# Two attention blocks on one core: block A's finished rows are transposed by VectorE and a DRAM round trip instead of TensorE, and split by GpSimd

## The chip, the cores and the metric

The kernel runs on one core of one Trainium2 chip. TensorE (PE; its weight loads are shown apart as PEld), VectorE (DVE), ScalarE (ACT) and GpSimd (POOL) each work through a queue of instructions in order; SyncE (SP) issues nearly all DMAs, in order too. An instruction waits for what it reads, and everything queued behind it on its engine waits with it. The metric is the device time of one execution in microseconds, as the median of several runs; one more execution was profiled, and the profile's rows come from that one.

## The reference

Two attention blocks with the same shapes (one sequence of 2048 positions, width 640, 32 heads of 20), side by side in the output. Block A lets each position see eight earlier ones at a distance of two; block B is full attention.

```python
def _A_ref(x, wqkv, wo):                    # W, dil = 8, 2
    q, k, v = split_heads(x @ wqkv)
    idx = pos[:, None] - off[None, :]       # off = arange(8) * 2
    logits = einsum("bhsd,bhswd->bhsw", q, k[idx]) * Dh ** -0.5   # masked where idx < 0
    o = einsum("bhsw,bhswd->bhsd", softmax(logits), v[idx])
    return merge_heads(o) @ wo
def _B_ref(x, wqkv, wo):
    q, k, v = split_heads(x @ wqkv)
    o = softmax(q @ k.T * Dh ** -0.5) @ v
    return merge_heads(o) @ wo
return concatenate([a, b], axis=-1)
```

## The kernel before

**Stages.** First come block A's projections (queries, keys and values go to DRAM), then block B's, then the main loop of 514 steps, in which block B's attention runs, and last block B's output projection. Block A's attention is computed by GpSimd beside block B's work, from the B projections on to about four fifths of the main loop.

**The main loop.** `NS = 512` steps are the combinations of 8 groups of four heads, 4 blocks of 512 queries and 16 blocks of 128 keys; `LAG = 2` more steps drain it. In step `i`, `b_qk(i)` makes four score tiles (TensorE into a PSUM bank each, of which there are four in the ring `bank()`; ScalarE's exponential to SBUF frees the bank); `b_pv(i - 2)` multiplies the exponentials of an earlier step by the values; and `b_max(i + 24)` makes the scores of a later query block once more, transposed, in two pairs of banks (`wide()`, a ring of two), and VectorE takes each row's maximum (tile `mx`, two `TENSOR_REDUCE` a step). TensorE may fill a `wide()` pair only when VectorE has read what stood in it. Every second step ScalarE copies the accumulated values into one of four `more` buffers and GpSimd adds them to `braw`. For steps in `ALONE` (432 to 479) the order within a step differs (`b_both`).

**Program order.** Everything is issued in the order of the Python program (`InOrder`, line 56, keeps it; so every row of the profile carries line 56, and tiles tell them apart). `tick()` at the start of a step counts `now` up and runs what `after(n, fn, ...)` has put down for this step. `odd(n)` moves a time to an odd step of the loop; VectorE's small operations (`sm`, `mx1`, `am`, `mtr`) stand on odd steps.

**Block A's attention.** `UNITS` is a list of 128 units: for each of the `NT = 16` tiles of 128 rows, four units for the scores (`a_scores`) and four for the values (`a_values`); the four score units of tile t + 1 come ahead of the four value units of tile t. `a_work` does one unit per `next`, in the loop at `i % 14` in (1, 5, 7, 11), so eight units, one tile, in 28 steps; 13 units are done ahead of the loop. The tile's softmax (`a_softmax`) proceeds by one part with each unit; its reciprocal `am` on VectorE comes with the second unit after the last value unit of the tile before. The finished rows of a tile are `ao`, [128 rows, 640], and go into `done_a` with a count of 2 that goes down with each unit.

**Block A's output projection.** TensorE contracts over partitions, so the rows have to be turned: `aot` holds them as [128 columns, part, 5 chunks, 128 rows], in two parts, a rounded one and the rest (`hi` and `lo`), of which three products are added (`rows15`: 15 matmuls for 320 output columns). `out_piece()` runs in the loop at `i % 6 == 4` and does one piece of `a_out`: first the turn (five transposes by TensorE into a `wide()` pair, ScalarE's cast to `aot[:, 0]`, VectorE's subtraction to `aot[:, 1]`), then one half of the projection, then the other; so three pieces, 18 steps, a tile. When the last tile is out, the weights of block B's output are loaded (`WO_b`), which take the buffers of A's.

**Buffers.** `stg` is a ring of three tiles of [128, 640] that weights and loads are staged through; `aot` has one buffer.

Of the kernel before, what the change touches and what calls it, by code (L numbers as in the profile page):

```python
# [8 lines left out]
F32 = mybir.dt.float32  # L9
F32R = mybir.dt.float32r  # L10
AF = mybir.ActivationFunctionType
ALU = mybir.AluOpType
AX = mybir.AxisListType

D = 640
# [5 lines left out]
KC = 5  # L21
# [38 lines left out]
def attention_pair(ctx, tc, xa, wqk_a, wv_a, wo_a, xb, wqk_b, wv_b, wo_b, oa, ob):  # L60
# [3 lines left out]
    sb = ctx.enter_context(tc.tile_pool(name="sb", bufs=1))  # L64
    ps = ctx.enter_context(tc.tile_pool(name="ps", bufs=1, space=PS))
    dr = ctx.enter_context(tc.tile_pool(name="dr", bufs=1, space=bass.MemoryType.DRAM))
    pe, dve, act, gp, sp = (InOrder(tc, e) for e in (nc.tensor, nc.vector, nc.scalar, nc.gpsimd, nc.sync))


    now = [0]  # L70
    due = {}

    def after(n, fn, *args):
        due.setdefault(now[0] + n, []).append((fn, args))
# [7 lines left out]
    def tick():  # L82
        now[0] += 1
        for fn, args in due.pop(now[0], ()):
            fn(*args)
# [5 lines left out]
    def bank():  # L91

        n = free.pop(0)
        t = ps.tile([128, 512], F32, tag=f"st{n}", bufs=1, name="ps_st")
        taken[id(t)] = (n, t)
        return t

    def give(t):

        free.append(taken.pop(id(t))[0])  # L100

    def wide():

        return ps.tile([128, 2, 512], F32, tag="mx", bufs=2, name="ps_mx")
# [44 lines left out]
    def x_pieces(x, n, second=None):  # L149

        t = columns(n)
        src = x[:, n * 512:(n + 1) * 512].rearrange("(k p) c -> p k c", p=128)

        def piece(a, b):
            u = t[a // (KC - 1)]
            m = a % (KC - 1)
            split(u[:, 0, m:m + b - a], u[:, 1, m:m + b - a], src[:, a:b], "p", second)
        return t, [lambda a=a, b=b: piece(a, b) for a, b in PAIRS]

    def wide_pieces(src, second=None):  # L160

        w = [sb.tile([128, KC, 320], F32R, tag="w", bufs=4, name="ww") for _ in range(2)]
        return w, [lambda a=a, b=b: split(
            w[0][:, a:b], w[1][:, a:b], src[:, a:b], second=second, first=second and gp.tensor_copy) for a, b in PAIRS]
# [52 lines left out]
    def rows15(p, o, W):  # L217

        for k in range(KC):
            for i, (wi, xi) in enumerate(PASSES):  # L220
                pe.matmul(p[:, :320], o(xi, k), W[wi][:, k], start=(k == 0 and i == 0), stop=(k == KC - 1 and i == 2))
# [20 lines left out]
    def store_rows(p, dst):  # L242
        r = sb.tile([128, 320], F32, tag="r", bufs=3, name="ro")
        act.copy(r, p[:, :320])
        if id(p) in taken:
            give(p)
        after(1, sp.dma_start, dst, r)


    NT = S // 128  # L250
# [11 lines left out]
    t, more = x_pieces(xa, 1)  # L262
# [6 lines left out]
    for n in (2, 3):  # L269
        t, more = x_pieces(xa, n)  # L270
        XA.append(t)
        loads += more
    ident = const.tile([128, 128], F32, name="ident")
# [23 lines left out]
    UNITS = []  # L297
# [69 lines left out]
    next_a = [0]  # L367
    done_a = []

    def a_attention():  # L370
# [3 lines left out]
        for n, (t, c) in enumerate(UNITS):  # L374
# [17 lines left out]
            next_a[0] = n + 1  # L392
            yield

    def a_out(W):

        while done_a and done_a[0][0] <= 0:
            _, t, o = done_a.pop(0)
            ot = sb.tile([128, 2, KC, 128], F32R, tag="aot", bufs=1, name="aot")
            p = wide().rearrange("p b c -> p (b c)")  # L400
            for k in range(KC):
                pe.transpose(p[:, k * 128:(k + 1) * 128], o[:, k * 128:(k + 1) * 128], ident)
            pv = p[:, :D].rearrange("p (k c) -> p k c", c=128)
            act.copy(ot[:, 0], pv)
            dve.tensor_tensor(ot[:, 1], pv, ot[:, 0].bitcast(F32), ALU.subtract)
            yield
            for half in range(2):
                p = bank()
                rows15(p, lambda xi, k: ot[:, xi, k], W[half])
                store_rows(p, oa[t * 128:(t + 1) * 128, half * 320:half * 320 + 320])  # L410
                yield

    a_work = a_attention()
# [9 lines left out]
    for n in range(NA):  # L423
        nxt = None
        for t in range(NT):
            if n == 0 and t < 4:
                p = first[t]
            else:
                p = next(banks)
# [31 lines left out]
    def b_pieces(g):  # L461
        k = sb.tile([128, 2, S], F32R, tag="big", bufs=4, name="bk")
        q = sb.tile([128, NQC, 2, 512], F32R, tag="big", bufs=4, name="bq")
        v = sb.tile([128, NKB, VG], F32, tag="vb", bufs=2, name="vb")
        stacks[g] = (q, k, v)
        out = []
        hs = [slice(g * GH + 2 * r, g * GH + 2 * r + 2) for r in range(2)]

        def add(t, src, runs):
            for r0, s0, n in runs:  # L470
                out.append(lambda: sp.dma_start(t[r0:r0 + n].bitcast(F32), src[s0:s0 + n]))
        for r in range(2):
            for r0, s0, n in BK_RUNS:
                add(k[r * HALF:], kb_d[:, hs[r]], [(r0, s0, n)])
        for qc in range(NQC):
            for r in range(2):
                for r0, s0, n in BQ_RUNS:
                    add(q[r * HALF:, qc], qb_d[qc, :, hs[r]], [(r0, s0, n)])
        return out[:4], out[4:]

    def v_piece(g, b0, b1):

        sp.dma_start(stacks[g][2][:, b0:b1], vb_d[b0 * 128:b1 * 128, g * GH * VC:g * GH * VC + VG]
                     .rearrange("(b p) c -> p b c", p=128))
# [8 lines left out]
    for m in range(0, 10, 2):  # L493
        nxt = []
        for n in range(4):
            for j in range(2):
                p = next(banks)
# [4 lines left out]
                c = MS[m + j]  # L502
                o = (0, 1) if c < KC else (1, 0)
# [191 lines left out]
    def out_first(qc):  # L695

        o = columns(2)
        outs_b[qc] = o
        for k in range(KC - 1):
            after(1 + 2 * k, split, chunk(o, 0, k), chunk(o, 1, k),  # L700
                  ot_b[k * 128:(k + 1) * 128, qc * 512:(qc + 1) * 512], "stg", gp, gp.tensor_copy)
# [31 lines left out]
    for n in (2, 3, 0, 1):  # L733
        for half in range(2):
            for s in range(4 * n, 4 * n + 4):
                p = bank()
# [5 lines left out]
                c = 16 * VC + 11 * half  # L742
# [25 lines left out]
    WO, loads = [], []  # L768
# [10 lines left out]
    outs = iter(())  # L779
    fill = []  # L780

    def out_piece():

        nonlocal outs
        if next(outs, 0) is None:
            return True
        if done_a and done_a[0][0] <= 0:
            outs = a_out(WO)
            return next(outs, 0) is None
        return False  # L790

    WO_b = []
    loop[0] = now[0] + 1
    for i in range(NS + LAG):
        g, sub = divmod(i, NQC * NKB)
        if sub == 16 and g + 1 < NG:
            k_loads, q_loads = b_pieces(g + 1)
            for n, fn in enumerate(k_loads + q_loads + [lambda g=g + 1: v_piece(g, 0, NKB)]):
                after(1 + n, fn)
        if i in (NS - 56, NS - 40):  # L800
            out_first((i - NS + 56) // NKB)
        tick()
        if loads and i % 2:
            loads.pop(0)()
        if i % 14 in (1, 5, 7, 11) and next(a_work, 0) == 0:
            for d in done_a:
                d[0] -= 1
        if i // NKB in ALONE and i + LEAD < NS:
            b_both(i)
            if rows and i % 2:  # L810
                rows.pop(0)()
            b_pv(i - LAG)
            if fill and i % 2 == 0:
                fill.pop(0)()
            elif i % 6 == 4 and not out_piece() and len(UNITS) == next_a[0] and not WO_b:
                for h in range(2):
                    w, more = wide_pieces(wo_b[h], gp)
                    WO_b.append(w)
                    loads += more
            continue  # L820
        if i + LEAD >= NS:

            for _ in b_qk(i) if i < NS else ():
                pass
            if rows and i % 2:
                rows.pop(0)()
            if i % 2:
                b_pv(i - LAG - 1)
                b_pv(i - LAG)
                if fill:  # L830
                    fill.pop(0)()
            continue
        qk = b_qk(i) if i < NS else iter(())
        next(qk, None)
        if rows and i % 2:
            rows.pop(0)()
        if i >= LAG:
            b_pv(i - LAG)
        next(qk, None)
        mx = b_max(i + LEAD)  # L840
        next(mx, None)
        if fill and i % 2 == 0:
            fill.pop(0)()
        elif i % 6 == 4 and not out_piece() and len(UNITS) == next_a[0] and not WO_b:
            for h in range(2):
                w, more = wide_pieces(wo_b[h], gp)
                WO_b.append(w)
                loads += more
        next(mx, None)
# [16 lines left out]
    for n, p in enumerate(last):  # L866
        out_matmuls(p, qc, n, (KC - 1,))
        r = sb.tile([128, 320], F32, tag=("r", "p")[n > 1], bufs=(3, PB)[n > 1], name="ro")
# [38 lines left out]
```

## Time and profile before

| | us |
|---|---|
| median of 3 runs | 1861.09 (1859.49 to 1862.60) |
| the profiled execution | 1862.24 |
| its span, first to last instruction | 1860.4 |
| VectorE: row maxima `mx`, 1024 | 1201.3 |
| ScalarE: exponentials `e` from `ps_st`, 2000 | 1064.1 |
| GpSimd: all of block A's and the `braw` additions, busy in all | 1197.4 |
| TensorE: transposes of `ao`, 80 | 11.8 |
| ScalarE: cast to `aot`, 16 | 11.1 |
| VectorE: subtraction to `aot`, 16 | 13.2 |

Times in the groups are sums of busy time; an instruction's own duration is longer than its share of the queue where the next one begins before it has ended. TensorE's clock was granted in full nearly throughout (0.998). A row of the timeline gives the start in us from the span's start, the length, the engine, the operation and how many of it follow one another, and in brackets how long the engine was idle before and who released it. In rows of a group the two numbers behind the bar are the busy time in us and the mean of one in ns. Rows `engine <- who: us, times, longest` are waits.

### The profile page before, as it was taken

What the parts mean: (1) busy time and instruction counts of PE and PEld (TensorE: products, weight loads), DVE (VectorE), ACT (ScalarE), POOL (GpSimd) and SP (SyncE); (2) the same over time, 40 slices, a digit from 0 to 9 for tenths busy, and PEclk for the clock granted to TensorE, in tenths of its full rate; (3) what the DMA queues carried; (4) which work ended last, traced back from release to release, by engine and by line L of the source; (5) the groups of instructions that cost most, each with busy time, mean ns of one, the idle gap of its engine ahead of it and who ended that gap; (6) DMA issues with size and microseconds to landing.
All of it is one profiled execution on the core that took longest, in us unless ns stands there. A gap on an engine that the chain in (4) does not pass through costs nothing.

```text
span 1860.4 us, 30613 instructions
## 1 busy us (share of the span) xinstructions
PE 1815.9 (98%) x11323; PEld 981.7 (53%) x11323; DVE 1324.4 (71%) x1286; ACT 1374.7 (74%) x2669; POOL 1197.4 (64%) x998
## 2 busy tenths in 40 slices
PE   9999999999999999999999999999999999999999
PEld 8888888885443433434434334343443343433568
DVE  3000333278889899898898998989989988999400
ACT  4222322224889899898898998989989989999891
POOL 0000075048989898898988988989889762557332
PEclk9999999999999999999999999999999999999999
DMA  6333686645442254235234532642452322111123
GB/s 223 111 96 113 205 291 239 227 155 176 133 132 98 94 158 143 96 105 163 87 103 126 142 99 81 171 128 88 125 156 95 99 71 67 51 34 46 30 70 111
DMA packets 144110, 229.74 MB, mean 123 GB/s; under 512 B 43100, under 2 KB 74460, under 8 KB 142968
## 3 DMA queue, kind: packets, MB, share of 16 engines
q1 hardware_dynamic: 143384, 227.13, 39.7%
q8 instruction: 89, 1.46, 0.3%
q10 hardware_dynamic: 576, 0.66, 0.1%
q14 instruction: 61, 0.50, 0.1%
HBM read 168.05 MB, written 59.67 MB: 122 GB/s over the span
## 4 chain that ended last, share of the span: by engine, by line
PE 64%; DVE 25%; ACT 6%; issue 2%; POOL 1%; POOLq 0%; ACTq 0%
PE ps_st L56 45%; DVE mx L56 24%; PE ps_mx L56 20%; ACT e L56 4%; ACT more L56 1%; POOL akv L56 1%; DVE am L56 0%; DVE aot L56 0%; POOL braw L56 0%; ACT aot L56 0%; POOL ao L56 0%; DVE sm L56 0%; ACT braw L56 0%; POOL am L56 0%; POOL al L56 0%
## 5 line engine op out<-in xcount | busy, mean ns | idle before, releaser
L56 DVE TENSOR_REDUCE mx<-ps_mx 128x2 f32<-128x1024 f32 x1024 | 1201.3, 1220 | 144.4 <-PE ps_mx L56 138.5
L56 ACT ACTIVATE e<-ps_st 128x512 f32<-128x512 f32 x2000 | 1064.1, 615 | 50.9 <-PE ps_st L56 23.1
L56 PE MATMUL ps_st<-e,vb 128*32 128x512 f32 x4096 | 544.4, 606 | 1.2 <-ACT e L56 0.6
L56 PE MATMUL ps_st<-bq,bk 62*128 62x512 f32 x2000 | 491.6, 453 | 0.3
L56 PEld LDWEIGHTS ps_st<-bq,bk 62*128 62x128 f32 x2000 | 258.8, 184 | 431.7 <-ACT e L56 397.6
L56 POOL TENSOR_TENSOR braw<-braw,more 128x512 f32<-128x512 f32 x248 | 318.5, 1284 | 253.1 <-ACT more L56 250.4
L56 PE MATMUL ps_mx<-bk,bq 60*128 60x512 f32 x2048 | 442.7, 443 | 32.6 <-DVE mx L56 18.3
L56 POOL TENSOR_TENSOR akv<-akv,aq 128x1280 f32<-128x1280 f32 x64 | 188.2, 2941 | 236.5 <-DMA akv<-ka_d 236.5
L56 PEld LDWEIGHTS ps_mx<-bk,bq 60*128 60x128 f32 x2048 | 205.3, 185 | 180.4 <-DVE mx L56 167.7
L56 POOL TENSOR_TENSOR akv<-akv 128x640 f32<-128x640 f32 (+3 forms) x304 | 282.1, 928 | 23.8
L56 PEld LDWEIGHTS ps_st<-e,vb 128*32 128x32 f32 x4096 | 82.1, 108 | 154.2 <-ACT e L56 89.9
L56 ACT COPY more<-ps_st 128x512 f32<-128x512 f32 x248 | 150.5, 607 | 12.7 <-PE ps_st L56 6.2
L56 ACT COPY ro<-ps_st 128x320 f32<-128x320 f32 (+1 forms) x92 | 43.6, 474 | 155.7 <-PE ps_st L56 110.4
L56 POOL TENSOR_TENSOR akv<-akv,al 128x1280 f32<-128x1280 f32 x64 | 151.5, 2366 | 0.2
L56 PE MATMUL ps_st<-ww,xn 128*128 128x320 f32 x720 | 119.8, 314 | 0.0
L56 PEld LDWEIGHTS ps_st<-ww,xn 128*128 128x128 f32 x720 | 106.7, 188 | 19.8 <-ACT e L56 8.7
L56 POOL TENSOR_TENSOR xn<-stg,xn 128x512 fp32r<-128x512 f32 (+1 forms) x20 | 30.1, 1507 | 92.4 <-ACT xn L56 91.1
L56 DVE TENSOR_TENSOR wc<-stg,wc 128x480 fp32r<-128x480 f32 (+5 forms) x15 | 8.4, 558 | 102.0 <-ACT wc L56 102.0
L56 PE MATMUL ps_st<-ww,aot 128*128 128x320 f32 x480 | 78.8, 316 | 0.0
L56 POOL TENSOR_TENSOR ao<-ao,akv 128x640 f32<-128x640 f32 x48 | 74.7, 1556 | 3.8
L56 PEld LDWEIGHTS ps_st<-ww,aot 128*128 128x128 f32 x480 | 70.4, 188 | 11.3 <-ACT e L56 10.3
L56 ACT COPY ro<-ps_mx 128x480 f32<-128x480 f32 x32 | 18.0, 562 | 72.6 <-PE ps_mx L56 63.1
(85 smaller groups left out, 1295.4 us busy)
## 6 DMA issues: line engine op xcount, KB each, us to landing
akv<-ka_d SPq DMA_DIRECT2D x128, 320.0 KB
akv<-va_d SPq DMA_DIRECT2D x128, 320.0 KB
kb_d<-pr SPq DMA_DIRECT2D x20, 512.0 KB
qb_d<-pr SPq DMA_DIRECT2D x20, 512.0 KB
bk<-kb_d SPq DMA_DIRECT2D x16, 640.0 KB
bq<-qb_d SPq DMA_DIRECT2D x64, 160.0 KB
rb<-s_d SPq DMA_DIRECT2D x128, 64.0 KB
stg<-xb SPq DMA_DIRECT2D x12, 512.0 KB
```

What stands on the lines that cost most here:

```text
L56: return lambda *a, **k: self.tc.keep_in_program_order(op(*a, **k))
```

## The change

TensorE, the `wide()` pair, ScalarE and PSUM are no longer used for the turn. Two units after a tile's last (`a_turn`), VectorE transposes its five chunks of [128, 128] within blocks of 32x32, one chunk in each of the next five steps, into a `stg` tile. SP stores this to DRAM (`tr_d`) two steps later, and another three steps later loads it into a second `stg` tile with four DMAs, one for each 32 partitions, which put the blocks where they belong, in pieces of 32 elements (128 bytes). From three steps after that, `turn_parts` lets GpSimd make both parts of `aot`, if the one before is used up. Seven steps on, the two halves may be projected, at `i % 6 == 4` as before; a tile now takes two such pieces and not three. `left_a` counts the 32 halves, and block B's output weights are loaded when it is at zero.

```diff
+    left_a = [2 * NT]
+    turned = []
+    ready_a = []
+
+    def a_turn(t, o):
+        b = sb.tile([128, KC, 128], F32, tag="stg", bufs=3, name="turn")
+        d = dr.tile([128, D], F32, tag="tr_d", bufs=2, name="tr_d")
+
+        def back():
+            r = sb.tile([128, KC, 128], F32, tag="stg", bufs=3, name="back")
+            src = d.rearrange("(b j) (k m c) -> m j k b c", b=4, k=KC, c=32)
+            for m in range(4):
+                sp.dma_start(r[32 * m:32 * m + 32].rearrange("j k (b c) -> j k b c", c=32), src[m])
+            turned.append((now[0] + 3, t, r))
+        for k in range(KC):
+            after(1 + k, dve.transpose, b[:, k], o[:, k * 128:(k + 1) * 128])
+        after(KC + 2, sp.dma_start, d, b.rearrange("p k c -> p (k c)"))
+        after(KC + 5, back)
+
+    def turn_parts():
+        if ready_a or not turned or turned[0][0] > now[0]:
+            return
+        _, t, r = turned.pop(0)
+        ot = sb.tile([128, 2, KC, 128], F32R, tag="aot", bufs=1, name="aot")
+        gp.tensor_copy(ot[:, 0], r)
+        gp.tensor_tensor(ot[:, 1], r, ot[:, 0].bitcast(F32), ALU.subtract)
+        ready_a.append((now[0] + 7, t, ot))
+
     def a_out(W):
-        while done_a and done_a[0][0] <= 0:
-            _, t, o = done_a.pop(0)
-            ot = sb.tile([128, 2, KC, 128], F32R, tag="aot", bufs=1, name="aot")
-            p = wide().rearrange("p b c -> p (b c)")
-            for k in range(KC):
-                pe.transpose(p[:, k * 128:(k + 1) * 128], o[:, k * 128:(k + 1) * 128], ident)
-            pv = p[:, :D].rearrange("p (k c) -> p k c", c=128)
-            act.copy(ot[:, 0], pv)
-            dve.tensor_tensor(ot[:, 1], pv, ot[:, 0].bitcast(F32), ALU.subtract)
-            yield
+        while ready_a and ready_a[0][0] <= now[0]:
+            _, t, ot = ready_a[0]
             for half in range(2):
+                if half:
+                    ready_a.clear()
                 p = bank()
                 rows15(p, lambda xi, k: ot[:, xi, k], W[half])
                 store_rows(p, oa[t * 128:(t + 1) * 128, half * 320:half * 320 + 320])
+                left_a[0] -= 1
                 yield
...
-        if done_a and done_a[0][0] <= 0:
-            outs = a_out(WO)
-            return next(outs, 0) is None
-        return False
+        outs = a_out(WO)
+        return next(outs, 0) is None
...
         if i % 14 in (1, 5, 7, 11) and next(a_work, 0) == 0:
             for d in done_a:
                 d[0] -= 1
+        if done_a and done_a[0][0] <= 0:
+            a_turn(*done_a.pop(0)[1:])
+        turn_parts()
...
-            elif i % 6 == 4 and not out_piece() and len(UNITS) == next_a[0] and not WO_b:
+            elif i % 6 == 4 and not out_piece() and not left_a[0] and not WO_b:
```

More of the change, by code (lines that the diff above doesn't have):

```diff
@@ L843, in attention_pair @@
             fill.pop(0)()
-        elif i % 6 == 4 and not out_piece() and len(UNITS) == next_a[0] and not WO_b:
+        elif i % 6 == 4 and not out_piece() and not left_a[0] and not WO_b:
             for h in range(2):
```

## The prediction

> **What bounds the kernel now.** The page first, then the chain of waits in the middle of the main loop, then VectorE's timeline there.
>
> ```profile
> span 1860.4 us, 30613 instructions
> PE 1815.9 (98%) x11323; PEld 981.7 (53%) x11323; DVE 1324.4 (71%) x1286; ACT 1374.7 (74%) x2669; POOL 1197.4 (64%) x998
> PE 64%; DVE 25%; ACT 6%; issue 2%; POOL 1%; POOLq 0%; ACTq 0%
> 1173.80:1344.40 170.60, 164.85 (x1107) 67.76 (x1103) 155.27 (x148) 155.75 (x304) 150.70 (x126) 1.00 0.41 121
> ```
>
> The last line is a stretch of the main loop: 170.60 us long, with PE, PEld, DVE, ACT and POOL busy 164.85, 67.76, 155.27, 155.75 and 150.70. No engine is idle for long, so shares alone decide nothing. The chain does (start, length, what):
>
> ```profile
> 1177.90 2.37 DVE mx L56 x2
> ...
> 1180.31 0.49 PE ps_mx L56 x2
> 1180.81 1.75 PE ps_st L56 x12
> 1182.55 0.25 PE ps_mx L56 x2
> ...
> 1182.83 2.37 DVE mx L56 x2
> ```
>
> Two loop steps make one round: two row maxima on VectorE (2.37 us) free a PSUM pair, TensorE refills it, does the scores and values of a step (2.49 us together), and VectorE starts again, 4.93 us later. VectorE has two more maxima to do beside TensorE's part of the round, and then waits. Its timeline:
>
> ```profile
> 1172.97 4.68 DVE L56 TENSOR_REDUCE mx<-ps_mx 128x2 f32<-128x1024 f32 x4 [0.25 <-PE ps_mx L56]
> ...
> 1192.58 3.58 DVE L56 TENSOR_REDUCE mx<-ps_mx 128x2 f32<-128x1024 f32 x3 [0.24 <-PE ps_mx L56]
> ```
>
> Four undisturbed rounds lie between these starts: 19.61 / 4 = **4.90 us a round**, of which VectorE waits 0.25. What is put on VectorE in a round is free up to that gap and lengthens the round beyond it. Three existing small operations show the rate:
>
> ```profile
> 1232.79 4.69 DVE L56 TENSOR_REDUCE mx<-ps_mx 128x2 f32<-128x1024 f32 x4 [0.68 <-PE ps_mx L56]
> 1237.39 0.62 DVE L56 TENSOR_REDUCE am<-al 128x32 f32<-128x256 f32 x1
> 1237.93 4.60 DVE L56 TENSOR_REDUCE mx<-ps_mx 128x2 f32<-128x1024 f32 x4
> 1242.46 0.23 DVE L56 RECIPROCAL sm<-sm 128x16 f32<-128x16 f32 x1
> 1242.62 0.15 DVE L56 TENSOR_REDUCE mx<-mx 128x16 f32<-128x64 f32 x1
> 1242.77 2.36 DVE L56 TENSOR_REDUCE mx<-ps_mx 128x2 f32<-128x1024 f32 x2
> ```
>
> The 0.62 us reduction is followed 0.54 us later: a small operation takes its duration less 0.08 of VectorE's queue. Its round took 1237.93 - 1232.79 = 5.14, so 0.24 over 4.90. The next round took two operations in 0.31 us of queue and lasted 4.84: free. So the room is 0.25 + 0.08 = **0.33 us a round**, and 0.54 - 0.33 = 0.21 agrees with the 0.24.
>
> **What is removed.** One event per row tile: five TensorE transposes into a PSUM pair that the maxima need, ScalarE's cast, VectorE's subtraction. First the row that counts the events and times their last part (least, median, longest ns), then VectorE's timeline around one of them:
>
> ```profile
> L56 DVE TENSOR_TENSOR aot<-ps_mx,aot x16: 824/824/826, 458.5 to 1551.2; 128x640 fp32r<-128x640 f32 x16
> ```
>
> ```profile
> 1267.53 4.67 DVE L56 TENSOR_REDUCE mx<-ps_mx 128x2 f32<-128x1024 f32 x4 [0.26 <-PE ps_mx L56]
> 1272.12 0.34 DVE L56 RECIPROCAL am<-am 128x32 f32<-128x32 f32 x1
> 1272.45 3.56 DVE L56 TENSOR_REDUCE mx<-ps_mx 128x2 f32<-128x1024 f32 x3
> 1276.46 0.82 DVE L56 TENSOR_TENSOR aot<-ps_mx,aot 128x640 fp32r<-128x640 f32 x1 [0.45 <-ACT aot L56]
> 1277.20 6.09 DVE L56 TENSOR_REDUCE mx<-ps_mx 128x2 f32<-128x1024 f32 x5
> ...
> 1283.52 4.68 DVE L56 TENSOR_REDUCE mx<-ps_mx 128x2 f32<-128x1024 f32 x4
> ```
>
> From 1272.45 to 1283.52 there are two rounds and one event: 11.07 - 2 x 4.90 = 1.27 us. With the neighbouring round of 4.92 (1267.53 to 1272.45) as measure it is 1.23. I take 1.25: 16 x 1.25 = **20.0 us** go. All three parts sit in series on the round (transposes, then cast, then subtraction, while the next maxima have one PSUM pair less), so all of it is gained; what is late next is the round itself, at 4.90, as in the undisturbed rows. The two half projections of each tile stay: 32 before and after.
>
> **What VectorE gets.** Five transposes of 128x128 a tile, one in each of the five steps after the turn begins: 80. No transpose on VectorE is in this trace. The nearest rows:
>
> ```profile
> L56 DVE TENSOR_TENSOR wd<-stg,wd 128x128 fp32r<-128x128 f32 x2 | 0.6, 284 | 0.0
> L56 DVE TENSOR_TENSOR wd<-stg,wd 128x256 fp32r<-128x256 f32 x5 | 2.1, 418 | 0.0
> L56 DVE TENSOR_REDUCE mx<-mx 128x16 f32<-128x64 f32 x32 | 5.4, 167 | 0.1
> L56 DVE RECIPROCAL am<-am 128x32 f32<-128x32 f32 x16 | 5.5, 341 | 0.0
> ```
>
> ```profile
> L56 DVE RECIPROCAL sm<-sm x32: 235/243/256, 513.8 to 1826.0; 128x16 f32<-128x16 f32 x32
> ```
>
> Low end: the 167 ns of half as many elements, 0.09 of queue. High end: the reciprocal's price per element, (341 - 243) / 16 = 6.1 ns, which gives 243 + 112 x 6.1 = 926 ns, 0.85 of queue. I take the row of the same shape, 284 ns, so **0.20 us of queue**.
>
> The steps come as pairs (even, odd) of one round: the five fall on rounds of 2, 2 and 1. The block's own reciprocal (0.34 us, 0.26 of queue) comes four steps after the turn begins, in the second round. Beyond the room: 2 x 0.20 - 0.33 = 0.07; 2 x 0.20 + 0.26 - 0.33 = 0.33; 0. That is 0.40 a tile, 16 x 0.40 = **6.4 us** lost. Two corrections of about 2 us cancel: by the step numbers half of the tiles meet another small operation (0.31 us of queue) in one of their rounds, 8 x 0.31 = 2.5 more; and every tile has one of its rounds together with a half projection, after which VectorE waits 0.68 instead of 0.25 (the row of 1232.79), so that round's 0.07, 0.33 or 0 in turn is free, about 2.1 less. The low end gives 2 x 0.09 + 0.26 - 0.33 = 0.11, 1.8 us; the high end 1.37 + 1.63 + 0.52 = 3.52, 56 us.
>
> The Trainium skill, "VectorE: DVE Perf Modes", section "The three transpose paths", gives 311 ns for a bf16 128x128 on VectorE, in 32x32 blocks; no run here shows it. By it the sum would be an estimated 0.23 of queue, 0.13 + 0.40 + 0 a tile, 8.5 us instead of 6.4.
>
> **What GpSimd gets.** The two parts, off the PSUM path, and with rows of the same shapes:
>
> ```profile
> L56 POOL CAST ww<-stg 128x640 fp32r<-128x640 f32 x8 | 5.8, 720 | 5.0 <-PE ps_mx L56 3.5 <-DMA stg<-wo_a 1.5
> L56 POOL TENSOR_TENSOR ww<-stg,ww 128x640 fp32r<-128x640 f32 x8 | 12.4, 1553 | 0.6
> ```
>
> 0.72 + 1.55 = 2.27 us a tile, 36 us in all. I cost it at nothing: a tile comes every 28 steps, 14 rounds or 68.6 us and more, in which GpSimd is idle 12% (busy 150.70 of 170.60), 8.0 us. If that cover were gone, 36 us would land on the path.
>
> **SP and the DMAs.** Five more transfers a tile: one store of 320 KB, four loads in pieces of 128 bytes (2560). Neither a wait nor such pieces stand on the path before, so bounds:
>
> ```profile
> q1 hardware_dynamic: 143384, 227.13, 39.7%
> SPq L56 <- DMA s_d<-braw: 68.0, 31, 7.6
> SPq L56 <- POOL braw L56: 111.5, 32, 12.1
> 1272.08 0.32 SPq L56 DMA_DIRECT2D sm<-s_d  x1
> ```
>
> By bytes (227.13 MB in 39.7% of the span) 320 KB take 1.1 us; by packets (82 ns each, 16 engines) 2560 take 13 us. I stay near the low end, since the pieces are small. The new wait is SP's, for the store to land before the loads are issued; behind it stand the loads of the next keys and values, fetched two units ahead, and sometimes the load that VectorE's reciprocal of the sums waits for. That load is issued at 1272.08, and the reciprocal stands just ahead of the maxima of 1283.52, some 11 us later; SP's like wait for s_d is 2.2 us on average and 7.6 at most. So nothing there. VectorE also newly waits for the finished rows:
>
> ```profile
> 1257.00 1.56 POOL L56 TENSOR_TENSOR ao<-ao,akv 128x640 f32<-128x640 f32 x1
> ```
>
> They are done at 1258.56. By the step numbers that tile's turn begins with the round ahead of the one at 1267.53, so at 1262.6, and its first transpose stands a step later: over 4 us.
>
> **Sum.** Profiled execution 1862.24 (span 1860.4 and 1.84 around it): 1862.24 - 20.0 + 6.4 = 1848.6. The median of the three runs, 1861.09, lies 1.15 lower, so **1847.5 us**.
>
> **Rivals.**
>
> *Two passes.* 4-byte data may take VectorE twice as long: the 418 ns row, 0.34 of queue. 0.35 + 0.61 + 0.01 = 0.97 a tile, 15.5 us: 1862.2 - 20.0 + 15.5 - 1.15 = 1856.6. Against it: between the 128x128 and the 128x256 row an element of four bytes costs 134 / 128 = 1.05 ns, and nothing in the rows shows a second pass.
>
> *The long chain is late.* Transposes, store, loads, GpSimd and then TensorE, whose first matmul of a half now waits for GpSimd. GpSimd starts 13 steps after the turn began, 8 after the last transpose (20 us), and TensorE comes 7 steps (17 us) later. For it: SP's waits of up to 12.1 us and the 13 us bound on the loads can add up to 25. Each microsecond by which it is late costs 16; from 0.85 us a tile the gain is gone. With 1 to 2 us late: 1864 to 1880.
>
> *VectorE and GpSimd block each other* (slower than before). A transpose reads and writes SBUF alone; if it had to wait for GpSimd's running instruction, then with GpSimd busy 88% and instructions of 1.20 us on average (150.70 / 126), each would wait half of one in 88 of 100 cases, 0.53 us. Queue 0.73: 1.13 + 1.39 + 0.40 = 2.92 a tile, 46.7 us: 1862.2 - 20.0 + 46.7 - 1.15 = 1888. It decides from 0.40 of queue (5 x 0.40 + 0.26 - 3 x 0.33 = 1.27, the event's price), so from a wait of 0.2 us. Against it: the reciprocal sm, an SBUF operation with one input, took 235 to 256 ns in its 32 runs, most of them beside a busy GpSimd. The Trainium skill, "SBUF — State Buffer", section "SBUF: two separate sides", states this as a rule: VectorE in a two-port mode and GpSimd lock each other out for a whole instruction. Whether a transpose is such an operation no run here shows; by the rule the time would be that of this rival. The reciprocal's price per element, with no wait, ends here too: 1862.2 - 20.0 + 56 - 1.15 = 1897.
>
> **Chances.** Forecast 0.65 (1841 to 1853), two passes 0.13, long chain late 0.10, VectorE far dearer 0.08, the rest unnamed. About 0.2%, 3.7 us, is what a measurement here can tell from no change, so the bounds are 1857.4 and 1864.8: faster takes the forecast, most of two passes and a little of the late chain, **0.77**; same 0.10; slower 0.13. The range reaches from free transposes (1862.2 - 20 - 1.2 = 1841) over two passes to **1860**.
>
> **What would show it.** VectorE: a transpose of about 284 ns that does not stretch; rounds of 4.9 to 5.3 us where the transposes fall, and no event of 1.25 us between them. ScalarE and VectorE without aot; GpSimd with it, 0.72 and 1.55, busy some 91% in the loop. No wait of TensorE for GpSimd at aot, none of GpSimd for the turned rows. Wrong, if transposes take over 0.48 us (queue 0.40), if TensorE waits for aot, or if the rounds stay above 4.9 without VectorE.

## The result, and the profile after

| | before | changed |
|---|---|---|
| median | 1862.55 us (6 runs, 1859.49 to 1863.00) | 1847.43 us (6 runs, 1845.78 to 1849.53) |
| profiled execution | 1862.24 us | 1849.53 us |

The ratio is 0.9924, 95% interval 0.9914 to 0.9933: 0.76% faster. Against its own profiled execution the prediction had 1848.6, 0.9 below the one measured.

The page of the changed kernel, and the window of the same 64 steps that was shown of before (us, then busy PE, PEld, DVE, ACT, POOL):

```profile
span 1847.8 us, 30664 instructions
PE 1805.9 (98%) x11243; PEld 970.8 (53%) x11243; DVE 1320.7 (71%) x1350; ACT 1363.9 (74%) x2653; POOL 1233.1 (67%) x1030
...
q1 hardware_dynamic: 187672, 237.62, 42.3%
```

```profile
1161.70:1333.30 171.60, 167.42 (x1122) 70.61 (x1118) 154.70 (x157) 154.36 (x302) 157.14 (x131) 1.00 0.43 124
```

GpSimd took over 36 us: 1197.4 before, 1233.1 now, and in this window it is busy 157.14 of 171.60, 92%. The stretch is not shorter than the one of before (170.60): a window of a fixed number of steps holds more or fewer half projections, so what the change brought can't be read from one window. The DMA engines moved 44288 packets more on q1 for 2.6 points more of their time.

The new operations, by tile (shortest, median, longest ns):

```profile
L56 DVE STREAM_TRANSPOSE turn<-ao x80: 251/300/303, 446.7 to 1522.5; 128x128 f32<-128x128 f32 x80
L56 POOL CAST aot<-back x16: 712/719/727, 483.1 to 1552.0; 128x640 fp32r<-128x640 f32 x16
L56 POOL TENSOR_TENSOR aot<-back,aot x16: 1552/1558/1566, 483.9 to 1552.8; 128x640 fp32r<-128x640 f32 x16
```

The 284 ns and the 720 and 1553 ns that were taken from rows of the same shapes came out at 300 and at 719 and 1558. A tile's five transposes on VectorE's timeline:

```profile
1253.59 2.36 DVE L56 TENSOR_REDUCE mx<-ps_mx 128x2 f32<-128x1024 f32 x2 [0.65 <-PE ps_mx L56]
1255.86 0.30 DVE L56 STREAM_TRANSPOSE turn<-ao 128x128 f32<-128x128 f32 x1
1256.08 2.32 DVE L56 TENSOR_REDUCE mx<-ps_mx 128x2 f32<-128x1024 f32 x2
1258.32 0.29 DVE L56 STREAM_TRANSPOSE turn<-ao 128x128 f32<-128x128 f32 x1
1258.54 2.32 DVE L56 TENSOR_REDUCE mx<-ps_mx 128x2 f32<-128x1024 f32 x2
1260.78 0.29 DVE L56 STREAM_TRANSPOSE turn<-ao 128x128 f32<-128x128 f32 x1
1260.99 2.32 DVE L56 TENSOR_REDUCE mx<-ps_mx 128x2 f32<-128x1024 f32 x2
1263.23 0.29 DVE L56 STREAM_TRANSPOSE turn<-ao 128x128 f32<-128x128 f32 x1
1263.45 0.31 DVE L56 RECIPROCAL am<-am 128x32 f32<-128x32 f32 x1
1263.68 2.29 DVE L56 TENSOR_REDUCE mx<-ps_mx 128x2 f32<-128x1024 f32 x2
```

A transpose takes 0.22 us of VectorE's queue (1255.86 to 1256.08). The idle 0.25 ahead of every fourth maximum is gone: the transposes stand in it. The first round, with two of them, takes 1258.54 - 1253.59 = 4.95, the second, with two and the reciprocal, 5.14, against 4.90 undisturbed. The prediction had 4.97 and 5.23.

Something else is new. SP's timeline, and VectorE's a little later:

```profile
827.95 8.90 SPq L56 DMA_DIRECT2D back<-tr_d  x4
836.89 1.21 SPq L56 DMA_DIRECT2D bk<-kb_d  x1
...
847.01 0.34 SPq L56 DMA_DIRECT2D sm<-s_d  x1
```

```profile
841.93 4.71 DVE L56 TENSOR_REDUCE mx<-ps_mx 128x2 f32<-128x1024 f32 x4 [0.25 <-PE ps_mx L56]
848.70 0.25 DVE L56 RECIPROCAL sm<-sm 128x16 f32<-128x16 f32 x1 [2.06 <-DMA sm<-s_d]
...
848.95 4.60 DVE L56 TENSOR_REDUCE mx<-ps_mx 128x2 f32<-128x1024 f32 x4
```

Here the four loads of a turned tile fall among the loads of the next group of heads (`bk`) and hold SP for 8.90 us, while the DMA engines are busy 74% (820 to 837). The transfers behind them come later, VectorE waits 2.06 us for the sums' load, and the round takes 7.02 us (848.95 - 841.93); at the same step of before (856.23) that wait was not there. TensorE stops too, for 1.30 us, and from 852 to 854 the clock granted to it was 0.50 and not 1.00. In all VectorE's waits for that load are small, 3.9 us before and 5.9 now.

### The profile page after: what moved, and what is told of

Same layout as the page of the kernel before. It is cut to its first block, busy times and chain, and to the rows that moved or that the text cites. A ratio compares the mean times of both kernels' runs of the same rounds, so it can differ in the third digit from the quotient of the medians.

```text
span 1847.8 us, 30664 instructions
## 1 busy us (share of the span) xinstructions
PE 1805.9 (98%) x11243; PEld 970.8 (53%) x11243; DVE 1320.7 (71%) x1350; ACT 1363.9 (74%) x2653; POOL 1233.1 (67%) x1030
## 3 DMA queue, kind: packets, MB, share of 16 engines
q1 hardware_dynamic: 187672, 237.62, 42.3%
## 4 chain that ended last, share of the span: by engine, by line
PE 58%; DVE 23%; DMA 5%; ACT 5%; POOL 5%; issue 2%; SPq 1%; POOLq 0%; DVEq 0%; ACTq 0%
PE ps_st L56 40%; DVE mx L56 22%; PE ps_mx L56 18%; ACT e L56 4%; POOL akv L56 3%; ACT more L56 1%; SPq L56 1%; POOL braw L56 1%; DMA aq<-qa_d 1%; DMA akv<-va_d 1%; DMA s_d<-braw 1%; DMA akv<-ka_d 1%; DMA tr_d<-turn 1%; DVE am L56 0%; DVE turn L56 0%
```

## The experiments

All are timed against the kernel before, whose median on the same chips was 1860.5 to 1862.0; savings and losses between variants are differences of their medians. An interval on a ratio is some 0.13% wide on either side, 2.5 us, so a difference of two variants below some 3 us is not clear of none by itself.

**1. The event's price.** The kernel before without the turn:

```diff
+    kept = []
...
             _, t, o = done_a.pop(0)
-            ot = sb.tile([128, 2, KC, 128], F32R, tag="aot", bufs=1, name="aot")
+            if t == 0:
+                ot = sb.tile([128, 2, KC, 128], F32R, tag="aot", bufs=1, name="aot")
+                kept.append(ot)
...
+            ot = kept[0]
             yield
```

> The kernel before, with the turn (five TensorE transposes, cast, subtraction) made for the first tile alone; the other 15 tiles project that tile's aot again, so 15 events are left out and nothing takes their place. The prediction's theory: 15 x 1.25 = 18.8 us go, about 1843.8. Rival (the event fills time that the engines would lose anyway): well under half of it, 1853 or more.

Measured 1843.66 us, ratio 0.9905 (0.9891 to 0.9918), against 1861.94. 18.3 / 15 = **1.22 us an event** (1.0 to 1.35 by the interval); the prediction read 1.25 from two rounds of the timeline. That the whole price comes back when the event goes is shown.

**2. VectorE's transposes left out.** The rows are stored as they are.

```diff
-        b = sb.tile([128, KC, 128], F32, tag="stg", bufs=3, name="turn")
...
-        for k in range(KC):
-            after(1 + k, dve.transpose, b[:, k], o[:, k * 128:(k + 1) * 128])
-        after(KC + 2, sp.dma_start, d, b.rearrange("p k c -> p (k c)"))
+        after(KC + 2, sp.dma_start, d, o)
```

> The changed kernel with the 80 transposes on VectorE left out: the rows are stored to DRAM as they are, at the same steps; the four loads, GpSimd's parts and the projections stay. The prediction's theory: 6.4 us less than the changed kernel, 1841.0. Rival (VectorE's part costs about half of that, and the rest of what the change gives back is lost to SP and the DMAs): 1844 to 1845.

Measured 1845.30 us, ratio 0.9917 (0.9903 to 0.9931). 2.1 us below the changed kernel, not the 6.4 of the prediction; with the two intervals, anything from nothing to about 5.

**3. The four loads as one, in whole rows.**

```diff
-            src = d.rearrange("(b j) (k m c) -> m j k b c", b=4, k=KC, c=32)
-            for m in range(4):
-                sp.dma_start(r[32 * m:32 * m + 32].rearrange("j k (b c) -> j k b c", c=32), src[m])
+            sp.dma_start(r.rearrange("p k c -> p (k c)"), d)
```

> The changed kernel with one load of whole rows (2560 bytes a partition) in place of the four loads in pieces of 128 bytes, so the blocks are not put where they belong. The prediction's theory (SP and the DMAs cost nothing): no change, 1847.4. Rival (SP held by the four loads, VectorE then waits for the sums' load): 3 to 4 us less, 1843 to 1844.5.

Measured 1845.50 us, ratio 0.9914 (0.9900 to 0.9928): 1.9 us less, smaller than the rival's 3 to 4 and not clear of none. What the loads cost SP is clear. The issue of one, changed kernel and then this one (shortest, median, longest ns):

```profile
L56 SPq DMA_DIRECT2D back<-tr_d x64: 584/645/4788, 463.1 to 1532.9; - x64
```

```profile
L56 SPq DMA_DIRECT2D back<-tr_d x16: 320/371/745, 463.4 to 1528.1; - x16
```

Four times 645 ns, and up to 4788 for one, against one of 371.

**4. Every transpose twice.**

```diff
             after(1 + k, dve.transpose, b[:, k], o[:, k * 128:(k + 1) * 128])
+            after(1 + k, dve.transpose, b[:, k], o[:, k * 128:(k + 1) * 128])
```

> The changed kernel with every transpose issued twice in the same step, 160 in all. The prediction's theory with the 0.20 us of queue: the room of 0.33 us a round is used up by the first, so 5 x 0.20 = 1.0 us a tile less what is left of the room, 13 to 16 us more, 1860 to 1864. Rival (VectorE has more room than 0.33 a round): under 8 us more. Rival (a transpose waits for GpSimd): over 25 us more.

Measured 1866.37 us, ratio 1.0028 (1.0017 to 1.0038): slower than before, 18.9 us over the changed kernel, a little more than the 13 to 16 expected. VectorE's timeline of the same tile:

```profile
1269.97 0.64 DVE L56 STREAM_TRANSPOSE turn<-ao 128x128 f32<-128x128 f32 x2
1270.53 2.32 DVE L56 TENSOR_REDUCE mx<-ps_mx 128x2 f32<-128x1024 f32 x2
...
1275.57 0.64 DVE L56 STREAM_TRANSPOSE turn<-ao 128x128 f32<-128x128 f32 x2
1276.13 0.31 DVE L56 RECIPROCAL am<-am 128x32 f32<-128x32 f32 x1
1276.36 2.29 DVE L56 TENSOR_REDUCE mx<-ps_mx 128x2 f32<-128x1024 f32 x2
```

Two take 0.56 of queue (1269.97 to 1270.53), and the round 1276.36 - 1270.53 = 5.83. The first 80 transposes cost about 2 us (at most some 5), the second 80 cost 19: room on VectorE exists, is small, and the change uses nearly all of it.

**5, 6, 7. Better places.** One transpose a round and none in the reciprocal's round (the edit shown); the four loads in four successive steps; both.

```diff
-        for k in range(KC):
-            after(1 + k, dve.transpose, b[:, k], o[:, k * 128:(k + 1) * 128])
-        after(KC + 2, sp.dma_start, d, b.rearrange("p k c -> p (k c)"))
-        after(KC + 5, back)
+        for k, n in enumerate((1, 5, 7, 9, 11)):
+            after(n, dve.transpose, b[:, k], o[:, k * 128:(k + 1) * 128])
+        after(12, sp.dma_start, d, b.rearrange("p k c -> p (k c)"))
+        after(15, back)
```

> The changed kernel with the five transposes of a tile in five different rounds, none in the round of the block's reciprocal (steps 1, 5, 7, 9 and 11 after the turn begins); the store and the loads come five steps later. The prediction's theory (room of 0.33 us a round, of which one transpose takes 0.20): nearly the whole cost of VectorE goes, by the prediction's 6.4 us 1841, by the 2.1 us that the kernel without transposes showed 1845.3. Rival (the cost is not where they stand, but that they are there): no change, 1847.4.

> The changed kernel with the four loads of a tile issued in four successive steps instead of one, GpSimd three steps later. Theory from the kernel with whole rows (SP held by four loads in a row makes the transfers behind them late): up to 1.9 us less, 1845.5. Rival (the pieces of 128 bytes cost the same wherever they stand): no change, 1847.4.

> Both: one transpose a round and the loads in four successive steps. If both costs go and add up: 1847.4 - 2.1 - 1.9 = 1843.4. If neither goes: 1847.4.

Measured 1853.12 us (ratio 0.9958, 0.9946 to 0.9971), 1847.09 (0.9926, 0.9912 to 0.9939) and 1852.53 (0.9952, 0.9939 to 0.9964). The loads apart: no change. One a round: **5.7 us slower** than the change, which no theory had. The chain of the kernel with one a round, about step 25:

```profile
501.31 2.33 POOL akv L56
...
503.71 1.09 POOL akv L56
504.80 6.32 DMA s_d<-braw
...
511.13 1.54 DMA sm<-s_d
...
512.86 2.43 DVE mx L56 x3
```

VectorE's wait for the sums' load is 5.3 us in this one place, and TensorE, which waits for VectorE, stops for 4.59 us. Behind the stop the clock granted to it, the third number from the end of the row, is half of what the changed kernel had in the same stretch:

```profile
512.00:521.00 9.00, 6.46 (x27) 2.44 (x31) 6.39 (x9) 3.04 (x7) 7.48 (x8) 0.50 0.53 159
```

```profile
512.00:521.00 9.00, 9.00 (x62) 4.50 (x62) 7.56 (x10) 6.90 (x16) 8.53 (x9) 1.00 0.24 75
```

The first row is of one a round, the second of the change. Over the whole program TensorE is busy 4.2 us longer for the same 11243 instructions (1805.9 and 1810.1), so by this count much of the 5.7 us is the slower clock behind the wait; all five runs of experiment 5 had a mean clock of 0.995 or 0.996, the runs of the change 0.998 to 1.000. That the stop brings the lower clock is read from these places and not tested.

Why the sums come late is argued. The first tile's parts on GpSimd come together with the end of a query block and with the loads of the next group, and the block's sums are stored at 504.80; the store takes 6.32 us to land, with the DMA engines busy 54%. In the kernel before it took nearly as long (503.83 to the load's issue at 509.67), and VectorE, further behind there, did not wait. So the spacing matters less than how late a store goes out to a chain that VectorE waits for; what GpSimd and what the transfers add to that isn't separated.

**8. Twice the parts on GpSimd.**

```diff
-        gp.tensor_copy(ot[:, 0], r)
-        gp.tensor_tensor(ot[:, 1], r, ot[:, 0].bitcast(F32), ALU.subtract)
+        for _ in range(2):
+            gp.tensor_copy(ot[:, 0], r)
+            gp.tensor_tensor(ot[:, 1], r, ot[:, 0].bitcast(F32), ALU.subtract)
```

> The changed kernel with GpSimd's two parts made twice, so 2.27 us a tile or 36 us of GpSimd more in all. The prediction's theory (hidden while GpSimd has idle time: 8.0 us a tile before, 2.27 of it used): no change, 1847 to 1849. Rival (GpSimd is late already in the changed kernel and what it does shows on the path): 10 us more or up to 36, 1857 to 1883.

Measured 1852.17 us, ratio 0.9950 (0.9937 to 0.9962): 4.7 us more for 36 us of GpSimd. Between the two: most is hidden, not all.

**9. Neither transposes nor pieces.** Experiments 2 and 3 in one kernel.

> The changed kernel with both taken out: no transposes on VectorE, and one load of whole rows in place of the four loads in pieces. SP's store and load, GpSimd's parts and the projections stay. If the two costs add up (2.1 for the transposes, 1.9 for the loads): 1847.4 - 4.0 = 1843.4, and what lies above the kernel before without its 16 events (1843.7 - 1.25 = 1842.4) is GpSimd's and the store's. If both were one cost seen twice: 1845.4.

Measured 1844.02 us, ratio 0.9911 (0.9896 to 0.9926): 3.4 less than the change, near the sum of 4.0, at the edge of what can be told from none. Over the 1842.4 of a kernel without any event stay 1.6 us, for GpSimd, the store and the load; this is within the error.

**10. Spread, with the loads kept clear of the group's.**

```diff
+        i = now[0] - loop[0]
+        slow = 0 < t < NT - 2
+        steps = (1, 5, 7, 9, 11) if slow else (1, 2, 3, 4, 5)
...
+        n += 2
+        while slow and (i + n + 3) % (NQC * NKB) in range(14, 33):
+            n += 1
```

> The changed kernel, but for all tiles except the first and the last two: one transpose a round (steps 1, 5, 7, 9, 11), and the loads moved out of the steps in which SP loads the next group of heads (14 to 32 of every 64). The first tile, which lost 8 us in one place when it was spread, and the last two keep the change's steps. If VectorE's cost goes by the round and the loads only hurt beside the group's loads: 1847.4 - 2.1 - 1.9 = 1843.4, at worst 1846. Rival (what the spread kernel lost it lost everywhere): 1850 or more.

Measured 1846.46 us, ratio 0.9921 (0.9908 to 0.9933): not told apart from the change, and 6.7 below experiment 5. In its trace VectorE does not wait for the sums' load at the loop's start, and the clock is 1.00 from 512 to 521. That fits a loss at that one place, as the chain said; but the last two tiles and the loads were moved as well, so the place isn't isolated. The expected gain of 4 did not come.

**11, 12. What an event consists of.** The kernel before, its turn on TensorE; ScalarE copies to SBUF and GpSimd makes the parts, and a tile takes four pieces and not three (the second `yield`). First from the PSUM pair, then from two single banks:

```diff
-            act.copy(ot[:, 0], pv)
-            dve.tensor_tensor(ot[:, 1], pv, ot[:, 0].bitcast(F32), ALU.subtract)
-            yield
+            r = sb.tile([128, KC, 128], F32, tag="stg", bufs=3, name="back")
+            act.copy(r, pv)
+
+            def parts():
+                gp.tensor_copy(ot[:, 0], r)
+                gp.tensor_tensor(ot[:, 1], r, ot[:, 0].bitcast(F32), ALU.subtract)
+            after(1, parts)
+            yield
+            yield
```

> The kernel before, with the event cut short: TensorE's five transposes stay, ScalarE copies the PSUM pair to SBUF, and GpSimd makes both parts from there one step later; no VectorE, no DRAM. The prediction's theory (the three parts of an event stand in series on the round, 1.25 us, of which VectorE's subtraction is some 0.75): 16 x 0.75 = 12 us less than before, 1850. Rival (the PSUM pair and TensorE are what the event costs): 1856 or more. Rival (only VectorE's part counts): 1843.

```diff
-            p = wide().rearrange("p b c -> p (b c)")
-            for k in range(KC):
-                pe.transpose(p[:, k * 128:(k + 1) * 128], o[:, k * 128:(k + 1) * 128], ident)
...
+            for a, e in ((0, 4), (4, KC)):
+                p = bank()
+                for k in range(a, e):
+                    pe.transpose(p[:, (k - a) * 128:(k - a + 1) * 128], o[:, k * 128:(k + 1) * 128], ident)
+                act.copy(r[:, a:e], p[:, :(e - a) * 128].rearrange("p (k c) -> p k c", c=128))
+                give(p)
```

> The kernel with ScalarE's copy and GpSimd's parts (1868.2), but TensorE transposes into two single banks of the ring of four that the scores use, and the pair of banks of the row maxima is not touched; ScalarE copies in two pieces. If what an event costs is the pair that the maxima lose for its length (in the chain of the kernel before a third maximum of 1.2 us per event): most of the 1.25 goes, TensorE's 0.55 to 0.75 at most stays, 1849 to 1855. If the transposes and the copy cost as a series wherever they stand (1.45 an event): no change, 1866 to 1868.

Measured 1868.15 us, ratio 1.0036 (1.0024 to 1.0049), and 1860.02, ratio 0.9993 (0.9984 to 1.0002). With VectorE's 0.82 us gone from every event, the first is **slower** than before and the second the same. Only the rival of "1856 or more" covers 1868.15, and it had not said slower; in the second both forecasts missed. The chain at an event, of before, of the copy from the pair, and from single banks:

```profile
1272.46 3.56 DVE mx L56 x3
...
1276.07 0.50 PE ps_mx L56 x2
...
1280.93 2.36 DVE mx L56 x2
```

```profile
662.88 2.37 DVE mx L56 x2
...
665.38 0.75 PE ps_mx L56 x5
...
666.16 0.70 ACT back L56
```

```profile
666.21 0.24 PE ps_mx L56 x2
666.45 0.77 PE ps_st L56 x5
667.23 0.42 PE ps_mx L56
667.65 2.14 PE ps_st L56 x12
```

In the event of before that is shown three maxima stand on the chain, 3.56 us, where an undisturbed round has two, 2.37. The turn has one of the two pairs, so TensorE's next matmul of the maxima waits for the other, until the third maximum is done. So it is at six of the sixteen events. At the other ten the chain is the series that the prediction named, transposes, cast, subtraction, as in this one:

```profile
663.88 2.37 DVE mx L56 x2
...
666.38 0.75 PE ps_mx L56 x5
...
667.15 0.70 ACT aot L56
...
667.88 0.82 DVE aot L56
668.70 1.14 DVE mx L56
...
672.34 2.36 DVE mx L56 x2
```

Both paths are equally long: 672.34 - 663.88 = 8.46 over the series, 1280.93 - 1272.46 = 8.47 over the third maximum, between the same maxima of the loop. A part taken out of one of them should then leave the other as it is; this is inferred, and experiment 11, where a new wait appears, does not test it cleanly.

In experiment 11 TensorE waits for ScalarE's copy (0.75 + 0.70 and small gaps) at 15 of the 16 events, 11.7 us in all; why it waits for the copy there, and not for the third maximum as before, no run shows. In experiment 12 the pair is left alone, and yet (1860.02 - 1842.4) / 16 = 1.10 us an event stays, of which GpSimd's parts can be some 0.3 (experiment 8). At all sixteen events the transposes stand on the chain (0.77 to 0.79), and the scores behind them take 2.1 to 2.4 us instead of some 1.7. So the pair alone is not the price either. TensorE's own time is a large part: without 15 events (experiment 1) it was busy 1803.4 us and not 1815.9, 12.5 of the 18.5 us by which the span fell.

## Why the prediction was right

- *The event, 20.0 us.* Right in size: 1.22 x 16 = 19.5 by experiment 1. The reason given with it, that transposes, cast and subtraction stand in series, holds in the chain of ten of the sixteen events; at the other six a third maximum stands there, for the pair that the turn has taken, at the same length. The prediction read the size from the rounds and not from the parts, so it did not depend on which. What the parts are worth one by one it would have had wrong: the expectation of experiment 11, 12 us for the subtraction, failed. How the price divides between TensorE's time and the waits isn't settled; GpSimd had 36 us more in experiments 11 and 12, which experiment 8 prices at up to 4.7.
- *VectorE, 6.4 us.* Right in kind, too large: 2.1 by experiment 2, at most about 5. Duration (300 for 284 ns) and queue (0.22 for 0.20) were nearly right. The rule of 0.33 us of room holds roughly, and gives too much: 0.11 and 0.37 over for the two rounds shown, which had 0.05 and 0.24; with doubled transposes 1.05 for the round shown, which had 0.93. By these two rounds it would be 0.29 a tile, 4.6 us; what makes 2.1 of it, and whether the two corrections that were said to cancel do, is not shown.
- *A transpose's duration.* The Trainium skill, "VectorE: DVE Perf Modes", section "The three transpose paths", gives 311 ns for bf16 data; here 4-byte data took 251 to 303. The measurement decides, and the two-pass rival, with its 418 ns, falls.
- *VectorE and GpSimd blocking each other.* Falls: 80 transposes took between 251 and 303 ns beside a GpSimd that was busy 92%. The lock in the Trainium skill, "SBUF — State Buffer", section "SBUF: two separate sides", is stated for two-port modes and two inputs; these rows show no such wait for this operation.
- *GpSimd at nothing.* Nearly: 1.6 us, the store and the load included, is what experiment 9 leaves, within the error; and experiment 8 shows that the cover is not complete.
- *SP and the DMAs at nothing.* Probably too low by a small sum: about 1.9 us by experiment 3, not clear of none. VectorE's wait for the sums' load agrees with it, 3.9 us before, 5.9 with the change, 4.0 with whole rows. The issue of a load in pieces was not in the trace of before and was taken as cheap. The store also lands later than the 2.2 to 7.6 us of the wait it was compared with. The changed kernel's chain, about step 345:

```profile
1340.18 10.20 DMA tr_d<-turn
...
1350.44 0.64 SPq L56
...
1355.00 2.64 DMA sm<-s_d
1357.63 0.02 issue
1357.66 0.25 DVE sm L56
```

The late chain was a rival, but at another place: not TensorE waiting for `aot`, but VectorE for a small load queued behind SP's new transfers, here for 0.5 us.

So 20.0 - 6.4 = 13.6 stood for about 19.5 - 3.4 - 1.6 = 14.5, by experiments 1 and 9; the median fell by 15.1. The direction and most of the size were understood. That the forecast of 1847.5 came within 0.1 us of 1847.43 is luck: VectorE's cost was too high by about 4, what SP, the DMAs and GpSimd cost was left out, and the median of three runs from which it was reckoned, 1861.09, was 1.5 below that of six, 1862.55.

## What to carry to other kernels

Price an interruption of a tuned loop by the rounds around it, not by adding up its instructions: here two paths of the same length ran side by side, one over the instructions and one over the buffer that they held, and taking the subtraction out of the first gained nothing. Look at the chain of every event and not of one: sixteen alike in the program went two ways. Small work for a busy engine is free only up to the gap it has in each round, and full price beyond: the first 80 transposes cost 2 us, the second 80 cost 19. A detour through DRAM costs little where it is given time, but its issues stand in a queue with others, and a small load behind them that an engine waits for pays; where that stops TensorE, look at the granted clock of the next microseconds too.

## What was not expected of the hardware

A load of 80 KB in 640 pieces of 128 bytes occupied SP for 645 ns (median), a load of 320 KB in whole rows for 371. With other large loads in flight four of them held SP for 8.90 us, and an 8 KB store took 6.32 us to land. After TensorE had stood still for 4.59 us the clock granted to it was 0.50 from 512 to 521 (experiment 5), and after 1.30 us it was 0.50 from 852 to 854 (the change). The pieces themselves were cheap for the DMA engines: 44288 packets more took their share from 39.7% of 1860.4 to 42.3% of 1847.8 us, 43 us for 16 tiles or 2.7 a tile with the store, near the 2 x 1.1 us of store and load by bytes rather than the 13 by packets.
